# Batch 0 in two token halves: q and k by casting DMAs, and a first FFN block that begins on half its tokens

## The chip, the cores and the metric

One core of a Trainium2 chip. The metric is the device time of one launch in microseconds (us). Most runs of one kernel agree within 1%; all comparisons below are between runs of the state "fast", and a run that fell in the slower state (more than 1.5% above the fastest run of the same kernel) is named where it matters.

The kernel before had a median of 302.28 us (302.11 to 304.18, 3 runs). Over all rounds of this study, on several chips, it lay between 301.7 and 306.7 us, so each experiment is compared with the runs of the kernel before *of the same rounds*. Ratios are the mean time of one kernel's fast runs over that of the other's fast runs of the same rounds, so they are not quite the ratio of the medians quoted. Where two experiments of different rounds are compared by their times, chip and round differ too, and a difference of 1 us or less says nothing.

## The reference

```python
# B, H, S, Nb, D = 8, 8, 576, 16, 64 ; 4608 tokens, d_model 512, d_ff 768
k_all = concat([beacon_k, k], axis=2)          # 16 beacon columns, seen by every query
scores = q @ k_all.T / sqrt(D)                 # causal over the 576 own tokens
a = softmax(scores);  x = a @ v_all            # per batch and head
x = x.transpose(0, 2, 1, 3).reshape(B * S, H * D)
h = max(max(x @ w1, x @ w2), x @ w3)           # the FFN, three matrices in, maximum, one out
out = h @ w_out
```

(Cut: the set-up of the random inputs and the type conversions. Inputs and output are fp32.)

## The kernel before

Everything runs in bf16 on one core. Two heads are a *pair*, four pairs a batch, two pairs a *quad*. For each pair, q and k are loaded, cast, transposed on TensorE ("turned") and copied into `qT` and `kT`. The scores come in four groups; ScalarE (ACT) takes the exponentials, GpSimd or VectorE masks them, TensorE multiplies with v (PV) and with a column of ones. ACT inverts the sums (Ln, then Exp), VectorE multiplies into `xT`. The FFN takes blocks of 512 tokens: 22 units a block, 18 for w1, w2, w3 and 4 for w_out, doled out between the attention steps by a pacing formula. In batch 0 there is no FFN product to put between.

```python
def start():
    keep_busy(15)                              # dummy matmuls, to warm TensorE's clock
    next_load(); load_beacons(0, 1, bk32_0, nc.scalar); next_load(10)
    cast_piece(0, 0, by_dve); cast_piece(0, 1, by_act)
    ...                                        # turn pair 0, copy it out, turn the beacons
at_step(1, 0, C(cast_v, 0, 0, by_pool))        # GpSimd's work, by (pair, score group)
at_step(2, 0, L(load_w, 0, 0, d_ff))           # w0 asked for: after the start
...
at_step(4, 1, C(cast_v, 1, 0, by_pool))        # batch 1's values: cast here
at_step(4, 2, C(cast_v, 1, 1, by_pool))
at_step(5, 0, C(cast_pair, 7, by_pool, by_pool))
fine_at = {                                    # TensorE's work between batch 0's score groups
    (0, 0): [L(turn_apart, 1, 0)], (0, 1): [L(turn_apart, 1, 1)],
    ...
    (2, 0): [L(emit_pv, 0, 0, 0, 2)], (2, 1): [L(emit_pv, 0, 0, 2, 4), finish_pv],
    (2, 2): [L(keep_busy, 2, 320, True)],
    ...
    (4, 0): [L(turn_apart, 5, 0), L(turn_apart, 5, 1), L(emit_pv, 1, 0), finish_pv],
}
for p in range(NPAIR):                         # the loop, cut
    for s, gs in enumerate(steps(p)):
        ...                                    # scores, masks, PV
        if not fine and s == 0: place_beacons(p + 1, by_pool)
        emit_ffn(allowed)
        if not fine and s == 1: turn_pair(p + 1, by_act)   # in the PV banks
        ...
        finish_pv()
```

The softmax here doesn't subtract the row's maximum and nothing guards it: scores larger than these inputs give would overflow.

Of the kernel before, what the change touches and what calls it, by code (L numbers as in the profile page):

```python
# [16 lines left out]
def kernel(  # L17
# [13 lines left out]
    nc = tc.nc  # L31
# [17 lines left out]
    PR = 9  # L49
    PP = S // PR  # L50
    P_NINE = 4
# [18 lines left out]
    groups = [  # L70
# [5 lines left out]
    NG = len(groups)  # L76
    g_width = [sum(q1 - q0 for _, q0, q1 in pieces) for pieces in groups]
    g_base = [2 * sum(g_width[:gi]) for gi in range(NG)]
    AT_W = 2 * sum(g_width)
    assert max(g_width) <= 512  # L80
# [9 lines left out]
    st_pool = ctx.enter_context(tc.tile_pool(name="st", bufs=9))  # L90
    pair_pool = ctx.enter_context(tc.tile_pool(name="pair", bufs=3))
    v_pool = ctx.enter_context(tc.tile_pool(name="v", bufs=2))
# [25 lines left out]
    make_identity(nc, ident)  # L118
# [7 lines left out]
    for i in range(NT):  # L126
        z = const.tile([128, NKP], BF16, name=f"kT{i}")
        nc.vector.memset(z[:, NK:NKP], 0.0)
        kTs.append(z)
    nc.vector.memset(ones, 1.0)  # L130
    tri = const.tile([128, 128], BF16, name="tri")
    nc.gpsimd.memset(tri, 1.0)
    nc.gpsimd.affine_select(
        out=tri,
        in_=tri,
        compare_op=ALU.is_ge,
        fill=0.0,
        base=0,
        pattern=[[1, 128]],
        channel_multiplier=-1,  # L140
    )
# [19 lines left out]
    def load_pair(p, k_queue=None):  # L161
        b, g, j0 = place(p)
        hs = slice(head(g, j0), head(g, j0) + 2)
        st = new_stage(("pair", p))
        for i, (src, queue) in enumerate(((q, nc.sync), (k, k_queue or nc.sync))):
            if p < P_NINE:
                queue.dma_start(
                    out=st[:, i * PR * D : (i + 1) * PR * D],
                    in_=src[b, hs].rearrange("h (p r) d -> (h p) (r d)", r=PR),
                )  # L170
            else:
                queue.dma_start(
                    out=st[0:QP, i * NQ2 : (i + 1) * NQ2].rearrange("p (h x) -> p h x", h=2),
                    in_=src[b, hs].rearrange("h (p r) d -> p h (r d)", r=QR),
                )

    def cast_piece(p, i, cast):
        st = stage["pair", p]
        if p < P_NINE:
            t16 = pair_pool.tile([128, PR, D], BF16, name=f"t16{i}")  # L180
            cast(
                t16.rearrange("x r d -> x (r d)"), st[:, i * PR * D : (i + 1) * PR * D]
            )
        else:
            t16 = pair_pool.tile([QP, QR, 2, D], BF16, name=f"p16{i}")
            cast(  # L186
                t16.rearrange("p r h d -> p h r d"),
                st[0:QP, i * NQ2 : (i + 1) * NQ2].rearrange("p (h r d) -> p h r d", h=2, r=QR),
            )
        stage["pair16", p, i] = t16  # L190
# [63 lines left out]
    def turn_beacons(b0, b1, src):  # L254
        n = Nb * (b1 - b0)
        ps = ffn_psum.tile([128, PPB, n], BF16, name="fps")
        for pi in range(PPB):
            nc.tensor.transpose(
                ps[:, pi],
                src[:, 2 * pi : 2 * pi + 2].rearrange("p h d -> p (h d)"),  # L260
                ident[0:n, 0:n],
            )
        if b0 == 0:
            by_act(kTs[0][:, 0:Nb], ps[:, 0, 0:Nb])
        by_act(bT[:, :, Nb * b0 : Nb * b1], ps)
# [31 lines left out]
    def turn(p, i, ps):  # L297
        src = stage.pop(("pair16", p, i))
        if p >= P_NINE:
            for r in range(QR):  # L300
                nc.tensor.transpose(  # L301
                    ps[:, r * QP : (r + 1) * QP],
                    src[:, r].rearrange("p h d -> p (h d)"),
                    ident[0:QP, 0:QP],
                )
            return
        for r in range(PR):
            for e in range(2):
                hs = slice(64 * e, 64 * e + 64)
                nc.tensor.transpose(  # L310
                    ps[hs, r * PP : (r + 1) * PP],
                    src[hs, r],
                    ident[hs, hs],
                    tile_position=(64 * e, 64 * e),
                )

    def rows(p):
        return PR if p < P_NINE else QR

    def evac_q(p, ps, copy):  # L320
        copy(
            qTs[p % NT].rearrange("d (p r) -> d p r", r=rows(p)),
            ps.rearrange("d (r p) -> d p r", r=rows(p)),
# [6 lines left out]
    def evac_k(p, ps, copy):  # L330
        kT = kTs[p % NT]
        copy(  # L332
            kT[:, Nb:NK].rearrange("d (p r) -> d p r", r=rows(p)),
            ps.rearrange("d (r p) -> d p r", r=rows(p)),
# [9 lines left out]
    def turn_pair(p, q_copy):  # L344
        banks = [pv_bank(i, [128, 1024], BF16) for i in range(2)]
        for i in range(2):
            turn(p, i, banks[i][:, 0:S])
        evac_q(p, banks[0][:, 0:S], q_copy)
        evac_k(p, banks[1][:, 0:S], by_dve)
# [12 lines left out]
    def at_view(p, t, e, q0, q1):  # L362
        for gi, pieces in enumerate(groups):
            off = g_base[gi] + e * g_width[gi]
            for t_, lo, hi in pieces:
                if t_ == t and lo <= q0 and q1 <= hi:
                    return at[p][0 : k_rows[t], off + q0 - lo : off + q1 - lo]
# [3 lines left out]
    def both_heads(p, gi):  # L371
        W = g_width[gi]
        return at[p][:, g_base[gi] : g_base[gi] + 2 * W].rearrange("k (e c) -> k e c", e=2)

    def emit_scores(p, gi):
# [6 lines left out]
        for t, q0, q1 in groups[gi]:  # L382
# [12 lines left out]
            out=both_heads(p, gi), in_=ps[:, :, 0 : g_width[gi]], func=AF.Exp, scale=scale  # L395
        )

    def emit_masks(p, gi, dve=False):
        off = 0
        for t, q0, q1 in groups[gi]:  # L400
            n = k_rows[t]
# [28 lines left out]
    def emit_pv(quad, hf, first=0, last=len(passes), apart=False):  # L430
        b, g = divmod(quad, n_quad)
        v_sb = v_tiles[b]
        if first == 0:
# [6 lines left out]
        for part, bank, lo, ca, cb in passes[first:last]:  # L440
            qa, qb = hf * HALF + ca, hf * HALF + cb
            ts = [t for t in range(n_kt) if q_min[t] < qb]
            for t in ts:
                q0 = max(qa, q_min[t])
                for j in range(4):
                    lhsT = (
                        ones[0 : k_rows[t]]
                        if part == 0
                        else v_sb[0 : k_rows[t], t, head(g, j), part - 1 : D : 2]
# [12 lines left out]
    def finish_pv():  # L462
# [3 lines left out]
        b, g = divmod(quad, n_quad)  # L466
# [5 lines left out]
        c0 = b % RING * S + hf * HALF  # L472
        for part, bank, lo, ca, cb in passes[1:]:
# [5 lines left out]
        if g == n_quad - 1 and hf == 1:  # L479
            ready[0] = b  # L480
# [7 lines left out]
    def mm1_unit(tb, ft, i, pool, name):  # L488
        if ft == 0 and i == 0:
            hTs[tb] = ffn_h.tile([128, n_ft, TOKB], BF16, name="hT")  # L490
        hT = hTs[tb]
        ps = pool.tile([128, TOKB], FP32, name=name)
        c0 = tb * TOKB % (RING * S)
        n0 = min(TOKB, RING * S - c0)
        for x0, o0, n in ((c0, 0, n0), (0, n0, TOKB - n0)):
# [8 lines left out]
        if i == 0:  # L504
            (by_act if alone[0] else by_dve)(hT[:, ft, :], ps)  # L505
        else:
            nc.vector.tensor_max(hT[:, ft, :], hT[:, ft, :], ps)  # L507
# [23 lines left out]

    units = []
    for tb in range(n_tokb):
        last_b = (TOKB * (tb + 1) - 1) // S
        for i in range(3):
            for ft in range(n_ft):
                units.append((last_b, mm1_unit, (tb, ft, i)))
        for tt in range(TOKB // 128):
            units.append((last_b, mm2_unit, (tb, tt)))
    UPB = len(units) // n_tokb  # L540
    done = [0]

    def emit_ffn(limit, pool=None, name="fps"):
        if done[0] + 1 <= limit and done[0] < len(units) and units[done[0]][0] <= ready[0]:
            _, fn, args = units[done[0]]
            fn(*args, pool or ffn_psum, name)
            done[0] += 1
            return True
# [18 lines left out]
    loads = [L(load_pair, 0, nc.scalar), L(load_pair, 1, nc.scalar)] + load_pairs(2, 4)  # L567
    loads += [L(load_v, 0, 0), L(load_beacons, 1, B_PE, bk32_1), L(load_v, 0, 1)]
# [18 lines left out]
    def start():  # L587
        keep_busy(15)
        next_load()
        load_beacons(0, 1, bk32_0, nc.scalar)  # L590
        next_load(10)
        cast_piece(0, 0, by_dve)
        cast_piece(0, 1, by_act)
        stage.pop(("pair", 0))
        by_pool(bk16_0, bk32_0)
        next_load()
        q_ps = ffn_psum.tile([128, S], BF16, name="fps")
        k_ps = ffn_psum.tile([128, S], BF16, name="fps")
        turn(0, 0, q_ps)
        turn(0, 1, k_ps)  # L600
        evac_q(0, q_ps, by_act)
        evac_k(0, k_ps, by_dve)
        turn_beacons(0, 1, bk16_0)
        keep_busy(4)
        C(cast_pair, 1, by_pool, by_pool)()
# [5 lines left out]


    P_FINE = PPB + 1

    def steps(p):
        return [[gi] for gi in range(NG)] if p < P_FINE else [[0, 1], [2, 3]]

    at_step(0, 0, C(cast_pair, 2, by_pool, by_pool))
    at_step(0, 1, C(cast_pair, 3, by_pool, by_pool))
    at_step(1, 0, *[L(emit_masks, 0, gi) for gi in range(NG)])  # L620
    at_step(1, 0, C(cast_v, 0, 0, by_pool))
    at_step(1, 1, C(cast_v, 0, 1, by_pool))
    at_step(1, 2, L(by_pool, bk16_1, bk32_1))
    at_step(1, 3, C(cast_pair, 4, by_pool, by_pool))
    at_step(2, 0, L(load_w, 0, 0, d_ff))
    at_step(2, 2, C(cast_pair, 5, by_pool, by_pool))
    at_step(3, 2, C(cast_pair, 6, by_pool, by_pool))
    at_step(3, 3, L(load_w, 1, 0, d_ff))
    at_step(4, 1, C(cast_v, 1, 0, by_pool))
    at_step(4, 2, C(cast_v, 1, 1, by_pool))  # L630
    at_step(5, 0, L(load_w, 2, 0, d_ff))
    at_step(5, 0, C(cast_pair, 7, by_pool, by_pool))
    at_step(6, 0, L(load_w_out))
# [6 lines left out]

# [118 lines left out]
```

## Time and profile before

| | kernel before |
|---|---|
| median | 302.28 us |
| span in the profile, first to last instruction | 301.2 us |
| first exponential | 7.85 us |
| first FFN product | 31.48 us |
| end of FFN block 0 | 70.95 us |
| from there to the end | 230.25 us, TensorE busy 225.8 |

"End of FFN block 0" is the end of the fourth w_out unit in TensorE's timeline. It is a good mark: after it TensorE is full, so whatever a change of the start brings must show as an earlier mark. The lines of the profile are in the prediction.

### The profile page before, as it was taken

To read this page: it belongs to the slowest core of one execution; us is meant where nothing else is said; L and a number is where in the kernel's file an instruction comes from. 1 tells how busy PE (TensorE), PEld (TensorE's weight loads), DVE (VectorE), ACT (ScalarE), POOL (GpSimd) and SP (SyncE) were. 2 spreads that over 40 slices of the span, in tenths; PEclk is the share of its full clock that TensorE was granted. 3 is DMA by queue.
4 is the path that set the end of the run, shared out by engine and by line. 5 is a ranking of instruction groups with operands and counts; after the bars stand their busy time and mean duration, and the time that the engine had idled before them with its cause. 6 is when DMAs were issued, how large, how long until landed. Compare 5 with 4: busy or idle time off the path is not lost.

```text
span 301.2 us, 8622 instructions
## 1 busy us (share of the span) xinstructions
PE 285.2 (95%) x3563; PEld 147.8 (49%) x3563; DVE 174.2 (58%) x330; ACT 143.1 (48%) x220; POOL 128.6 (43%) x261
## 2 busy tenths in 40 slices
PE   7797849999999999999999999999999999999995
PEld 4454325454454545454445777545454544444442
DVE  2966525656766476646564656465646575275373
ACT  3786635573555464636463646354645531400300
POOL 3876294455666583465455543652243210000000
PEclk9979989999999999999999999999999999999999
DMA  7999999999899999999999999557512001103003
GB/s 258 211 255 216 208 239 239 216 227 216 177 311 180 265 223 262 191 188 253 291 202 177 249 236 201 113 141 209 115 44 104 2 2 70 72 0 116 25 2 139
DMA packets 83095, 51.55 MB, mean 171 GB/s; under 512 B 62064, under 2 KB 76656, under 8 KB 83056
## 3 DMA queue, kind: packets, MB, share of 16 engines
q1 hardware_dynamic: 80976, 47.23, 70.4%
q0 software_dynamic: 1648, 3.15, 5.5%
q8 instruction: 28, 0.46, 0.7%
q10 hardware_dynamic: 432, 0.62, 0.6%
q14 instruction: 11, 0.09, 0.1%
HBM read 35.13 MB, written 14.22 MB: 164 GB/s over the span
## 4 chain that ended last, share of the span: by engine, by line
PE 81%; DMA 9%; SPq 3%; DVE 2%; POOL 2%; issue 1%; ACT 0%; POOLq 0%; DVEq 0%
PE fps L497 41%; PE fps L514 13%; PE pv L451 11%; PE sc L385 8%; DMA st<-in_v_dram 5%; PE sc L497 5%; PE sc L514 2%; DMA st<-in_q_dram 2%; DMA st<-in_k_dram 2%; SPq L249 1%; SPq L213 1%; PE pv L301 1%; DVE kT L332 1%; POOL v_sb L229 1%; POOL at_sb L410 1%
## 5 line engine op out<-in xcount | busy, mean ns | idle before, releaser
L394 ACT ACTIVATE at_sb<-sc 128x992 bf16<-128x992 f32 (+3 forms) x128 | 103.5, 862 | 99.1 <-PE sc L385 99.1
L497 PE MATMUL fps<-xT,w_sb 128*128 128x512 bf16 (+1 forms) x648 | 140.2, 357 | 1.2 <-ACT at_sb L394 1.2
L497 PEld LDWEIGHTS <-w_sb 128*128 128x128 bf16 x720 | 65.8, 98 | 71.5 <-issue 15.4
L507 DVE TENSOR_TENSOR hT<-hT,fps 128x512 bf16<-128x512 bf16 x96 | 65.8, 686 | 46.0 <-PE fps L497 45.8
L410 POOL TENSOR_SCALAR_AFFINE_SELECT at_sb<-at_sb 128x256 bf16<-128x256 bf16 (+2 forms) x145 | 52.5, 384 | 90.7 <-ACT at_sb L394 89.2
L186 POOL CAST p<-st 96x768 bf16<-96x768 f32 x56 | 44.8, 825 | 9.2 <-DMA q_dram<-p 5.3
L514 PE MATMUL fps<-w_out_sb,hT 128*128 128x512 bf16 x180 | 41.8, 379 | 0.0
L505 DVE CAST hT<-fps 128x512 bf16<-128x512 f32 x42 | 29.0, 690 | 19.8 <-PE fps L497 19.7
L385 PE MATMUL sc<-qT,kT 64*128 64x288 bf16 (+4 forms) x384 | 35.8, 284 | 2.9 <-POOL kT L328 1.9
L522 DVE COPY y<-fps 128x512 f32<-128x512 f32 x30 | 20.7, 690 | 27.9 <-PE fps L514 25.1
L514 PEld LDWEIGHTS <-hT 128*128 128x128 bf16 x216 | 20.5, 98 | 25.0 <-DVE hT L507 1.3
L474 DVE TENSOR_TENSOR xT<-pv,recip 128x288 bf16<-128x288 f32 (+2 forms) x93 | 27.3, 349 | 4.6 <-ACT recip L471 4.4
L451 PE MATMUL pv<-at_sb,v_sb 128*32 128x192 bf16 (+4 forms) x1352 | 28.9, 232 | 0.0
L385 PEld LDWEIGHTS <-kT 64*128 64x128 bf16 x384 | 13.8, 94 | 27.9 <-issue 19.4
L451 PEld LDWEIGHTS <-v_sb 128*32 128x32 bf16 (+1 forms) x1408 | 24.9, 98 | 3.0 <-issue 1.9
L229 POOL CAST v_sb<-st 128x512 bf16<-128x512 f32 (+2 forms) x26 | 21.5, 844 | 9.8 <-DMA st<-in_v_dram 9.8
L451 PE MATMUL pv<-at_sb,ones 128*32 128x288 bf16 (+4 forms) x492 | 17.9, 258 | 2.9 <-POOL at_sb L410 2.1
L497 PE MATMUL sc<-xT,w_sb 128*128 128x512 bf16 x72 | 18.5, 379 | 0.0
L469 ACT ACTIVATE lnd<-pv 128x288 f32<-128x288 f32 x31 | 12.9, 415 | 8.2 <-PE pv L451 8.2
L451 PEld LDWEIGHTS <-ones 128*32 128x32 bf16 (+1 forms) x512 | 11.1, 96 | 10.2 <-issue 8.0
L507 DVE TENSOR_TENSOR hT<-hT,sc 128x512 bf16<-128x512 bf16 x12 | 8.3, 688 | 12.5 <-PE sc L497 12.2
L505 ACT CAST hT<-sc 128x512 bf16<-128x512 f32 x6 | 3.5, 586 | 23.7 <-PE sc L497 23.7
(47 smaller groups left out, 114.6 us busy)
## 6 DMA issues: line engine op xcount, KB each, us to landing
st<-in_q_dram SPq DMA_DIRECT2D x32, 288.0 KB, 5.7
out_dram<-y SPq DMA_DIRECT2D x36, 256.0 KB, 2.8
st<-in_k_dram SPq DMA_DIRECT2D x30, 288.0 KB, 6.1
st<-in_v_dram SPq DMA_DIRECT2D x24, 256.0 KB, 6.7
w_sb<-in_moe_w_dram POOLq DMA_DIRECT2D x6, 384.0 KB, 9.2
q_dram<-p SPq DMA_DIRECT2D x16, 144.0 KB, 2.6
k_dram<-p SPq DMA_DIRECT2D x16, 144.0 KB, 2.5
st<-in_v_dram SPq DMA_DIRECT2D x8, 224.0 KB, 6.4
```

The source lines that it names most:

```text
L186: cast(t16.rearrange("p r h d -> p h r d"), st[0:QP, i * NQ2 : (i + 1) * NQ2].rearrange("p (h r d) -> p h r d", h=2, r=QR),)
L229: cast(v_sb[0:n, t:t1].rearrange("p t h d -> p (t h d)"), st[0:n, (t - t_lo) * H * D : (t1 - t_lo) * H * D],)
L385: nc.tensor.matmul(ps[:, e, off : off + q1 - q0], kT[hs, 128 * t : 128 * t + 128], qT[hs, q0:q1], start=True, stop=True, tile_position=(64 ...
L394: nc.scalar.activation(out=both_heads(p, gi), in_=ps[:, :, 0 : g_width[gi]], func=AF.Exp, scale=scale)
L410: nc.gpsimd.affine_select(out=view, in_=view, compare_op=ALU.is_ge, fill=0.0, base=x0, pattern=[[0, 2], [1, hi - lo]], channel_multiplier=-1,)
L451: nc.tensor.matmul(ps[bank][32 * j : 32 * j + 32, lo + q0 - qa : lo + qb - qa], lhsT, at_view(PPQ * quad + j // 2, t, j % 2, q0, qb), star ...
L474: nc.vector.tensor_mul(xT[:, 2 * g + part - 1, c0 + ca : c0 + cb], ps[bank][:, lo : lo + cb - ca], recip[:, ca:cb],)
L497: nc.tensor.matmul(ps[:, o0 : o0 + n], w_in[i][:, ct, 128 * ft : 128 * (ft + 1)], xT[:, ct, x0 : x0 + n], start=(ct == 0), stop=(ct == n_c ...
L505: (by_act if alone[0] else by_dve)(hT[:, ft, :], ps)
L507: nc.vector.tensor_max(hT[:, ft, :], hT[:, ft, :], ps)
L514: nc.tensor.matmul(ps, hT[:, ft, 128 * tt : 128 * (tt + 1)], w_out_sb[:, ft, :], start=(ft == 0), stop=(ft == n_ft - 1),)
L522: nc.vector.tensor_copy(y, ps)
```

## The change

The intent is to fill the first 31 us, in which TensorE waits for exponentials and has no FFN product. Batch 0 is cut in two halves of 288 tokens. The first halves of all four pairs go first, so that x is complete for 288 tokens early and FFN block 0 can begin with half units (256 tokens of w1 and w2) while the second halves are still in attention. Most of batch 0's q and k, and w0 after them, come by casting DMAs on GpSimd's software queue, so no engine casts them (w0 came that way before too, but was asked for at 20.63 us). From pair 4 on the loop is also reordered: pairs are turned in a score bank instead of the PV banks, and the beacon columns are copied into `kT` by VectorE instead of GpSimd.

```diff
-    keep_busy(15)
-    next_load() ... cast_piece(0, 0, by_dve) ... turn(0, 0, q_ps)
+    keep_busy(12)
+    load_half(0, 0, nc.sync); load_half(0, 1, nc.scalar)
+    load_half(1, 0, nc.sync); load_beacons(0, 1, bk32_0, nc.scalar); load_half(1, 1, nc.scalar)
+    load_quad(1, 0); load_quad(0, 1); load_quad(1, 1)     # casting DMAs, GpSimd
+    load_w(0, 0, d_ff)                                    # w0, right behind them
+    next_load(9)                      # batch 0's values, beacons, pairs 4 to 6, batch 1's values, pair 7
 ...
+    first_steps = [
+        ((0, 0), [T(2, 0, False)]),
+        ((1, 0), [M(0, 0, True), T(3, 0, True), C(cast_v, 0, 0, by_pool)]),
+        ((2, 0), [M(1, 0), T(0, 1, False)]),
+        ((3, 0), [T(1, 1, True), M(2, 0, True), M(3, 0)]),
+        ((0, 1), [M(0, 1), L(load_w, 1, 0, d_ff)]),
+        ((0, 2), [T(2, 1, False), M(0, 2)]),
+        ((0, 3), [M(0, 3, True), P(0, 0)]),
+        ((1, 1), [M(1, 1), finish_pv]),
+        ((1, 2), [P(1, 0, True), M(1, 2)]),
+        ... ((2, 2), [M(2, 1), F(2), M(2, 2, True)]), ...  # F(2): two FFN half units
+    ]
 ...
-    at_step(4, 1, C(cast_v, 1, 0, by_pool)); at_step(4, 2, C(cast_v, 1, 1, by_pool))
+    at_step(5, 0, C(cast_v, 1, 0, by_pool)); ... at_step(5, 1, C(cast_v, 1, 1, by_pool))
 ...
+        if tb == 0:
+            spans = [(0, 0, 0, MID), (1, 0, 0, MID), (0, need, MID, TOKB), (1, need, MID, TOKB)]
 ...
-        if not fine and s == 0: place_beacons(p + 1, by_pool)
+                    place_beacons(p + 1, by_dve)
```

(Cut: the same idea carried through the loads, transposes, masks and score groups of batch 0, and the order of the loop. `T` turns a half pair, `M` masks, `P` is a PV product, `F(n)` emits n FFN half units, `C` is a GpSimd cast and the next load.)

## The prediction

> **What bounds the kernel now.** I read first the busy shares and the strip of 40 slices, to see which engine fills which part of the time.
>
> ```profile
> PE 285.2 (95%) x3563; PEld 147.8 (49%) x3563; DVE 174.2 (58%) x330; ACT 143.1 (48%) x220; POOL 128.6 (43%) x261
> ...
> PE   7797849999999999999999999999999999999995
> ...
> PEclk9979989999999999999999999999999999999999
> DMA  7999999999899999999999999557512001103003
> ```
>
> One slice is 7.5 us. TensorE is full from the seventh slice to the last; only the first six have holes. So I then cut the run into windows at the events that matter: first scores (7.4), end of the last exponential of batch 0 (24.9), first FFN product (31.48), the end of the holes (44.67), the end of FFN block 0 (70.95), the last product. Columns: window, its length, busy time of PE, PEld, DVE, ACT, POOL, granted clock, DMA share, GB/s.
>
> ```profile
> 0.00:7.40 7.40, 5.61 (x59) 3.16 (x59) 1.71 (x8) 2.88 (x5) 2.29 (x10) 1.00 0.76 255
> 7.40:24.90 17.50, 14.86 (x317) 8.83 (x316) 13.43 (x30) 14.25 (x22) 13.89 (x24) 0.90 1.07 231
> 24.90:31.48 6.58, 3.76 (x128) 2.45 (x129) 4.21 (x13) 4.22 (x9) 2.75 (x6) 1.00 1.13 216
> 31.48:44.67 13.19, 9.17 (x100) 4.38 (x100) 4.83 (x8) 6.09 (x9) 8.82 (x20) 0.93 1.08 226
> 44.67:70.95 26.28, 25.95 (x348) 12.99 (x344) 15.24 (x30) 14.51 (x23) 12.75 (x27) 0.97 1.13 230
> 70.95:297.50 226.55, 225.81 (x2620) 115.99 (x2620) 134.13 (x244) 101.13 (x156) 88.13 (x177) 1.00 0.69 153
> ```
>
> From 70.95 on, TensorE is busy 225.81 of 226.55 us: nothing is to be had there unless work is removed, and the change removes none. All the room is before 44.67, where ACT does the exponentials of batch 0 (14.25 busy of 17.5 us) and no FFN product runs until 31.48. The chain of waits up to 60 us says why: a load of batch 1's values, then GpSimd in its order.
>
> ```profile
> 19.76 15.94 DMA st<-in_v_dram
> 35.77 0.08 issue
> 35.85 1.46 POOL v_sb L229
> ...
> 40.15 0.14 POOL kT L328
> ```
>
> That load took 15.94 us. GpSimd waited for it, then had casts and masks to do before it copied the beacon columns into kT at 40.10. In the timeline TensorE is held by exactly these two things:
>
> ```profile
> 40.35 0.54 PE L385 MATMUL sc<-qT,kT 64*128 64x288 bf16 x8 [1.89 <-POOL kT L328]
> ...
> 43.31 0.57 PE L451 MATMUL pv<-at_sb,ones 128*32 128x176 bf16 x6 [2.11 <-POOL at_sb L410]
> ```
>
> **What the Trainium skill says.** (1) "DMA: Bandwidth & Descriptors", section SWDGE vs HWDGE vs iDMA: a cast during a DMA can be issued from GpSimd only, where software writes the descriptors. The trace agrees on the cost to GpSimd: the six casting weight loads took 528 to 673 ns of POOL each and 7.0 to 11.9 us to land. (2) The same page, Queues, rings and completion order: each DMA engine goes round-robin between its queues, a packet at a time. The trace fits: while four weight loads were under way, the value load beside them took 15.94 us against a median of 6.7. (3) "SBUF — State Buffer", Who interferes with whom: VectorE in a two-port mode and GpSimd exclude each other from a shared port for a whole instruction. The small copy into kT shows something like it: 186 to 194 ns on GpSimd, but 158, 518 (median) and 2169 ns on VectorE. (4) "TensorE: Matmul & The Clock Gate", Part 1: a quiet TensorE drops to half clock. The granted clock was 0.64 in the window 16 to 20 us.
>
> **The change part by part.**
> *Start.* Pairs 0 and 1 load half as much first (0.59 MB for both pairs instead of 1.18), so transposes can begin nearly 1 us earlier than 5.37. But VectorE now casts the beacons in its order, and they landed at 5.9; and pair 1's transposes stand ahead of pair 0's scores. First exponential: about 7.4 instead of 7.85.
> *Loads.* Pairs 2 and 3 and all second halves come by six casting DMAs (0.295 MB read each, 1.77 MB), then w0 (1.57 MB) behind them on the same queue; w0 had been asked for at 20.63. In 4 to 8 us before, with large runs alone, 380 GB/s arrived; w0 and w1 beside value loads took 14 us for 3.15 MB read, 225 GB/s. At 200 to 225 from 3 us on: the three quads land at about 7, 10 and 13 us, w0 at about 20, w1 at about 27. The first FFN product can thus run at 20 to 21 instead of 31.48. The six issues cost GpSimd about 6 x 0.65 = 4 us, at a time when it was waiting.
> *ACT in batch 0.* Two exponentials of 992 and 736 columns take 1.67 us in the timeline, 0.97 ns a column. Batch 0 has 3328 columns a pair, 3.2 us; four pairs 12.9. Three inversions (0.41 + 0.44 each) add 2.55: 15.4. ACT was busy 81% of the time in 7.4 to 24.9 before. The new order has more waits in it (TensorE's order puts each PV, which waits for masks and cast values, ahead of later scores, and the FFN products wait for w0 and for the first half of x). I choose 72%: 15.4 / 0.72 = 21.4, so the last exponential of batch 0 ends at 28.8 (24.9 before, with no FFN product among them). With the transposes of pair 4 and two FFN half units (1.2 us), **pair 4 starts at about 30**, with 4 of block 0's 22 units already done.
> *From pair 4 to the end of block 0*, all on TensorE, durations by start to start in the packed stretch: 6 x 0.48 + 5 x 0.45 scores = 5.1; 6 turns x 0.51 = 3.1; PV 3 x 1.61 + 2 x 0.79 = 6.4; FFN 14 units x 0.88 + 4 x 1.33 = 17.6. Sum 32.2. The stall at 38 to 43 goes: the beacon copy is now VectorE's, and batch 1's values are asked for in the start, needed about 12 us after pair 4. I leave 1 us for new waits. Block 0 ends at 30 + 32.2 + 1 = 63.2 against 70.95: **7.75 us earlier**.
> *After that* the pacing formula gives the same FFN units beside the same pairs (22 due at the end of pair 9's first step in both, 145.75 at the end of pair 31), so the 226.55 + 3.7 us that follow should stay. Turning pairs in the score banks instead of the PV banks, and multiplying later, only reorders; TensorE is full there, so I put it at 0 +- 1.5. 302.3 - 7.8 = **294.5 us**.
>
> **The rivals.**
> *A: the casting DMAs are the new wait.* They are small runs (768 bytes in), mixed with the values' 256-byte runs and with w0, behind six software issues. For it: DMA share is at 1 all through the start, and the total before w1 has landed is not smaller than before. Against: the first 4 MB need only some 10 to 11 us at 380 GB/s. If each quad is 4 us late, TensorE, which works in order, holds everything: pair 4 at 34 to 36, a time of 298 to 301.
> *B: VectorE and GpSimd block each other.* Batch 0 now gives VectorE the beacon copies, half-width evacuations and many masks, just while GpSimd casts values. For it: the 2169 ns copy. Against: before, VectorE made five such copies in this phase too. Worth 1 to 3 us: 296 to 298.
> *C: the gain is handed back between pair 4 and pair 10*, because w1, w2, w_out or batch 1's values are not there when TensorE comes sooner. w_out is issued behind pair 7's casts, at perhaps 38, took 13.7 us to land, and is needed at about 54. For it: the load side was full (DMA share 1.13 up to 70.95). Against: about 10 us of slack at w2. 3 to 6 us back: 297 to 300.
> *D: better than I think.* If ACT stays at 81% as before, pair 4 starts near 27.5: 291 to 292.
>
> **Range and chances.** A, B and C each take from the gain, D adds. I put the middle at 294.5 and 8 of 10 between 288.5 and 299.5. Faster by 2% means under 296.2: the middle passes it by only 1.7 us, so faster 0.67, within 2% 0.30. Slower by 2% would need the start to lose 6 us net, against one in which no FFN product runs for 31 us: 0.03.
>
> **What would show it right or wrong.** Right: first FFN product at 20 to 22 us, pair 4's scores at 28 to 32, end of block 0 at 61 to 66, then about 230 us of full TensorE to the end. A shows as TensorE or VectorE waiting for a transpose whose source is a quad tile, or for w0, before 25 us. B shows as kT copies of over 1 us on VectorE. C shows as TensorE waits on weights or on masks behind a load between 30 and 60 us. If the stretch after block 0 is not within 1.5 us of 230, the claim that the reordering is neutral is wrong.

## The result, and the profile after

The changed kernel took 312.49 us (312.07 to 312.99, 4 runs) against 303.23 (302.11 to 304.90, 4 runs) for the kernel before in the same rounds: ratio 1.0301, 95% interval 1.0240 to 1.0362. **It is 3% slower; the prediction said 2.6% faster.** (Its own output check is not on record; the kernels below, most of them edits of it, all gave correct results.)

First the page of the changed kernel: busy time of TensorE, then its strip, its clock and the DMA engines in 40 slices of 7.8 us.

```profile
PE 291.4 (94%) x3566; PEld 155.4 (50%) x3566; DVE 178.4 (57%) x363; ACT 144.4 (46%) x221; POOL 129.6 (42%) x257
...
PE   7848895998999999999999999999999999999994
...
PEclk9999999799999999999999999999999999999999
DMA  8999999993976899979997999878202000202003
```

The third slice now is at 4. Beware of the clock strip (the clock that the throttle granted to TensorE, in tenths of full speed): it shows full speed at the start, but the profile holds no clock record before 34.0 us. The durations tell another story, as will be seen. Next the windows of the changed kernel at the prediction's marks: first exponential, first FFN product, pair 4's scores, end of FFN block 0, end (columns as in the prediction).

```profile
0.00:8.55 8.55, 6.31 (x52) 3.38 (x54) 3.25 (x18) 2.48 (x6) 6.66 (x16) 1.00 0.90 156
8.55:28.27 19.72, 13.76 (x207) 7.35 (x207) 8.17 (x29) 11.03 (x16) 7.82 (x18) 1.00 1.12 215
28.27:40.18 11.91, 10.48 (x137) 6.79 (x138) 6.18 (x18) 4.47 (x8) 4.90 (x8) 1.00 1.17 224
40.18:81.61 41.43, 35.95 (x571) 22.47 (x572) 23.65 (x52) 25.26 (x38) 22.48 (x43) 0.96 0.97 196
81.61:311.10 229.49, 224.85 (x2609) 115.45 (x2608) 137.14 (x250) 101.19 (x155) 87.77 (x172) 1.00 0.63 149
```

The last row settles one thing: after block 0 the changed kernel needs 229.49 us, the kernel before 230.25. **The whole loss is ahead of that mark**, which moved from 70.95 to 81.61 us. Against the prediction the first FFN product is 7 us late (28.27 for 20 to 22), pair 4 is 10 us late (40.18 for 30), and the stretch from there to the end of block 0 took 41.43 us instead of 33.2.

Who made whom wait? In the chain of waits of the changed kernel one piece is far larger than any other; it is shown here with what follows it:

```profile
4.20 15.28 DMA st<-in_v_dram
19.48 0.05 issue
19.53 0.62 POOL v_sb L258
20.15 0.34 POOL at_sb L450
```

A load of batch 0's values ends at 19.48. GpSimd waits for it, and behind that cast, in the same queue, stand masks of the exponentials. In the timeline of the changed kernel TensorE's first PV product waits for exactly these masks:

```profile
20.53 0.85 PE L494 MATMUL pv<-at_sb,ones 128*32 128x288 bf16 x10 [4.28 <-POOL at_sb L450]
```

And ACT, which sets the pace of batch 0, waits for scores that stand behind this PV product in TensorE's order. The list of waits up to 36 us, "engine, what it could not start, for whom: total us, times, longest", for the kernel before and then for the changed one:

```profile
ACT at_sb L394 <- PE sc L385: 5.2, 5, 1.8
```

```profile
ACT at_sb L431 <- PE sc L422: 15.0, 7, 6.6
```

So ACT was busy 15.3 of the 29.1 us between the first and the last exponential of batch 0: 53%, where 72% was predicted.

A second new stall lies later, beside batch 1's value casts. First GpSimd's and then VectorE's timeline of the changed kernel, and what TensorE did:

```profile
49.48 1.46 POOL L258 CAST v_sb<-st 128x1536 bf16<-128x1536 f32 x1
50.89 1.60 POOL L215 CAST p<-st 96x768 bf16<-96x768 f32 x2
```

```profile
50.21 3.14 DVE L364 COPY kT<-bT 128x16 bf16<-128x16 bf16 x1
```

```profile
53.43 2.98 PE L553 MATMUL fps<-xT,w_sb 128*128 128x256 bf16 x16 [2.04 <-DVE hT L561]
```

The copy of 16 beacon columns, 153 ns at its shortest, took 3.14 us while GpSimd ran its casts and then issued w_out's load (52.44 to 53.29); the evacuation of an FFN bank stood behind it on VectorE, and TensorE waited 2.04 us for that bank.

### The profile page after: what moved, and what is told of

Same layout as the page of the kernel before. It is cut to its first block, busy times and chain, and to the rows that moved or that the text cites. A ratio compares the mean times of both kernels' runs of the same rounds, so it can differ in the third digit from the quotient of the medians.

```text
span 311.1 us, 8625 instructions
## 1 busy us (share of the span) xinstructions
PE 291.4 (94%) x3566; PEld 155.4 (50%) x3566; DVE 178.4 (57%) x363; ACT 144.4 (46%) x221; POOL 129.6 (42%) x257
## 4 chain that ended last, share of the span: by engine, by line
PE 84%; DMA 6%; DVE 5%; ACT 2%; issue 1%; POOL 0%; DVEq 0%; ACTq 0%
PE fps L553 33%; PE pv L494 13%; PE sc L553 12%; PE fps L570 11%; PE sc L422 8%; DMA st<-in_v_dram 5%; PE sc L570 4%; PE sc L329 2%; DVE kT L368 1%; DMA h<-in_q_dram 1%; DVE kT L364 1%; DVE y L578 1%; ACT at_sb L431 1%; DVE xT L526 1%; PE fps L494 1%
## 5 line engine op out<-in xcount | busy, mean ns | idle before, releaser
L431 ACT ACTIVATE at_sb<-sc 128x928 bf16<-128x928 f32 (+5 forms) x128 | 104.0, 861 | 102.9 <-PE sc L422 100.6
L553 PE MATMUL fps<-xT,w_sb 128*128 128x512 bf16 (+1 forms) x580 | 123.7, 347 | 4.4 <-DVE hT L561 2.3
L563 DVE TENSOR_TENSOR hT<-hT,fps 128x512 bf16<-128x512 bf16 (+1 forms) x82 | 52.8, 648 | 34.3 <-PE fps L553 33.8
L553 PE MATMUL sc<-xT,w_sb 128*128 128x512 bf16 (+1 forms) x188 | 43.1, 356 | 0.0
L422 PE MATMUL sc<-qT,kT 64*128 64x288 bf16 (+5 forms) x400 | 38.1, 294 | 2.0 <-ACT qT L357 2.0
L561 DVE CAST hT<-fps 128x512 bf16<-128x512 f32 (+1 forms) x44 | 26.9, 618 | 17.5 <-PE fps L553 17.5
L563 DVE TENSOR_TENSOR hT<-hT,sc 128x512 bf16<-128x512 bf16 x32 | 22.0, 688 | 16.6 <-PE sc L553 16.2
L494 PE MATMUL pv<-at_sb,v_sb 128*32 128x288 bf16 (+5 forms) x1376 | 30.1, 235 | 0.0
L494 PEld LDWEIGHTS <-ones 128*32 128x32 bf16 (+2 forms) x512 | 11.2, 98 | 12.6 <-issue 11.0
L570 PE MATMUL sc<-w_out_sb,hT 128*128 128x512 bf16 x60 | 14.8, 379 | 0.3 <-DVE hT L563 0.3
```

Source lines behind the costliest of these rows:

```text
L422: nc.tensor.matmul(ps[:, e, off : off + q1 - q0], kT[hs, 128 * t : 128 * t + 128], qT[hs, q0:q1], start=True, stop=True, tile_position=(64 ...
L431: nc.scalar.activation(out=both_heads(p, gi), in_=ps[:, :, 0 : g_width(p, gi)], func=AF.Exp, scale=scale)
L494: nc.tensor.matmul(ps[bank][32 * j : 32 * j + 32, lo + q0 - qa : lo + qb - qa], lhsT, at_view(PPQ * quad + j // 2, t, j % 2, q0, qb), star ...
L553: nc.tensor.matmul(ps[:, o0 : o0 + n], w_in[i][:, ct, 128 * ft : 128 * (ft + 1)], xT[:, ct, x0 : x0 + n], start=(ct == 0), stop=(ct == n_c ...
L561: (by_act if alone[0] else by_dve)(h, ps[:, 0 : hi - lo])
L563: nc.vector.tensor_max(h, h, ps[:, 0 : hi - lo])
```

## The experiments

Eighteen kernels ran, all with a correct result. Four theories of the loss were tried first:

- **Clock**: the first phase runs at half clock because its matmuls are sparse and there are only 12 dummies.
- **Values starved**: w0, asked for in the start, takes DMA time from batch 0's values.
- **Shared port**: VectorE's beacon copies collide with GpSimd's casts from pair 4 on.
- **Loop body**: turning pairs in a score bank brings new waits.

### Clock: warm, before12

`warm` adds dummy matmuls so that TensorE never cools before the first PV product:

```diff
-        keep_busy(12)
+        keep_busy(20)
-        ((0, 0), [T(2, 0, False)]),
+        ((0, 0), [T(2, 0, False), L(keep_busy, 5, 320, True)]),      # and in four more turns
-        ((0, 3), [M(0, 3, True), P(0, 0)]),
+        ((0, 3), [M(0, 3, True), L(keep_busy, 34, 320, True), P(0, 0)]),
```

> The changed kernel with 20 dummy products at its start (12), five more after each of five turns of batch 0, and 34 ahead of the first PV. Theory C (clock): TensorE never reached full clock before 33.6 us for want of dense work; with these it is at full clock by 6 us, the transposes of 96 columns fall from 283 to about 200 ns and the scores of 288 columns from 418 to 290 ns, the values' stall stays (first PV still ends its wait near 20.5), and 4 to 6 us are saved: 306.5 to 308.5. Theory V (only the values' load counts): less than 2 us saved, over 310.5.

Measured: 312.09 us, ratio 1.0275 (1.0224 to 1.0326). It saved 0.4 us. Up to the first PV product the clock did what was wanted. Twelve transposes in the changed kernel, then in `warm`, by TensorE's timeline:

```profile
10.39 0.69 PE L344 MATMUL pv<-ident,quad 96*64 96x96 bf16 x12
```

```profile
10.47 0.45 PE L344 MATMUL pv<-ident,quad 96*64 96x96 bf16 x12
...
17.43 4.79 PE L390 MATMUL fps<-busy 128*128 128x320 bf16 x34
22.15 0.52 PE L494 MATMUL pv<-at_sb,ones 128*32 128x288 bf16 x12
```

The mean duration of a score matmul of 288 columns was 418 ns in the changed kernel at 8 to 12 us and 293 ns in `warm`. Like matmuls stayed that long in the changed kernel (412 to 422 ns at 22 to 30 us) and took 293 ns from 34 us on. So it did run at half clock up to about 34 us, whatever its clock strip says. But the values were cast at 19.38 in `warm`, as late as before, and the first PV product came at 22.15. The time set free went into waiting. As the *first* cause, the clock falls. Later `warm` did not stay warm: at 28 to 30 us, with its first FFN products, its granted clock was 0.53.

`before12` takes three dummies out of the kernel before (`keep_busy(15)` to `keep_busy(12)`):

> The kernel before with 12 dummy products at its start instead of 15, nothing else. Theory C: three dummies decide the clock; it stays at half clock past 5 us, up to where the FFN makes it dense, transposes of 64 columns and scores of 288 columns (293 ns) become about 1.4 times as long, and the time rises by 2 to 5 us, to 305 to 308. If 12 are enough here, the time stays within 0.5% and the sparse work, not the dummies, is what keeps the changed kernel cold.

Measured: 303.84 us, ratio 0.9998 (0.9948 to 1.0049). Twelve dummies are enough there; it is the later, sparser work that lets the changed kernel stay cold, not their number (`sc_ahead_warm` below has 20 and none in the turns, and was at 0.51 at 12 to 16 us).

### Values starved: w0late, w0late_warm, quad_hw

`w0late` asks for w0 only after the cast of batch 0's first values:

```diff
         load_quad(1, 1)
-        load_w(0, 0, d_ff)
         next_load(9)
-        ((1, 0), [M(0, 0, True), T(3, 0, True), C(cast_v, 0, 0, by_pool)]),
+        ((1, 0), [M(0, 0, True), T(3, 0, True), C(cast_v, 0, 0, by_pool), L(load_w, 0, 0, d_ff)]),
```

> The changed kernel with w0's load issued after the casts of batch 0's first values and no longer ahead of them. Theory V: the third value tile lands near 14 to 15 us instead of 19.5, the first PV waits under 1 us, 3 to 5 us saved: 307.5 to 309.5, still at half clock. Theory C alone: the time is spent elsewhere at half clock, under 2 us saved.

Measured: 309.04 us, ratio 1.0175 (1.0123 to 1.0228), 3.4 us better than the changed kernel, as expected. GpSimd's and TensorE's timelines of `w0late`:

```profile
15.50 0.61 POOL L258 CAST v_sb<-st 128x512 bf16<-128x512 f32 x1 [3.26 <-DMA st<-in_v_dram]
```

```profile
17.63 0.84 PE L494 MATMUL pv<-at_sb,ones 128*32 128x288 bf16 x10 [1.08 <-POOL at_sb L450]
```

The third value cast came at 15.50 instead of 19.53, the wait of the first PV product fell from 4.28 to 1.08 us, and block 0 ended at 77.2 instead of 81.6. w0's early load cost more than it gave: no wait for w0 had been seen at all.

`w0late_warm` joins this with the dummies of `warm` (10 instead of 34 ahead of the first PV):

> Both together (10 dummies ahead of the first PV). If C and V are separate causes, the sum of their gains, 8 to 11 us: 302 to 305, as the kernel before. If they are the same gap seen twice, no better than the better of the two.

Measured: 309.05 us, ratio 1.0167 (1.0107 to 1.0227). A miss: the dummies added nothing even here. But this is no test of a start at full clock either: from 26 to 30 us `w0late_warm` ran at 0.50, and its pair 4 came at 37.54 us, that of `w0late` at 36.45.

`quad_hw` asks whether the software queue itself is at fault. It is `w0late`, but the quads come in fp32 on SyncE's hardware queue and GpSimd casts them:

```diff
-            nc.gpsimd.dma_start(out=t16..., in_=half_source(g, h, i, 0, 4))   # casts on the way
+            nc.sync.dma_start(out=st[0:QP, ...], in_=half_source(g, h, i, 0, 4))
+            by_pool(t16..., st[0:QP, ...])                                    # later
```

> w0late with the six casting DMAs replaced by loads of fp32 on the sync queue, in order with the values (quads 1 and 0's second half ahead of the first values, the last quad after them), cast on GpSimd. To be compared with w0late (309.0). Theory V in its narrow form (the software queue takes turns with the values' short runs and holds them back): the third value tile lands by 12 us instead of 15.5 and 1.5 to 3 us are saved, 306 to 307.5. If only the bytes count: within 1 us of 309.

Measured: 313.90 us, ratio 1.0321 (1.0281 to 1.0362), 4.9 us slower than `w0late`. The third value cast came at 15.25, hardly sooner than the 15.50 of `w0late`: the casting DMAs were not what still held the values back. The last quad was cast at 18.29 and TensorE waited 2.5 us for one of those casts. So of the two ways tried the casting DMAs are the better one; what delayed the values was w0 beside them.

### From pair 4 on: oldloop, beac_pool, w0late_oldloop

`oldloop` gives the changed kernel the loop body of the kernel before from pair 4 on (beacon copies on GpSimd, pairs turned in the PV banks, sums inverted and multiplied at the step's end). `beac_pool` takes back one line of it only:

```diff
-                        place_beacons(p + 1, by_dve)
+                        place_beacons(p + 1, by_pool)
```

> The changed kernel with the body of the loop from pair 4 on as it was before: beacon copies on GpSimd, pairs turned in the PV banks at a pair's second step, sums inverted and multiplied at the end of a step. Batch 0's start stays as changed. Theory L (the reordered loop is not neutral): in the changed kernel TensorE waits 0.34, 0.99, 0.30, 2.04, 0.34 and 1.30 us between pair 4 and the end of block 0, on copies out of the score banks and on a VectorE copy of 3.1 us, and falls to half clock once more; with the old body 4 to 6 us are saved, 306.5 to 308.5, and from pair 4's scores to the end of block 0 it takes 35 to 37 us instead of 41.4. If the loop is neutral, as the prediction had it, within 1 us of 312.5.

> The changed kernel with only the beacon copies of that loop back on GpSimd. Theory S (shared port): the 3.1 us copy on VectorE near 50 us is gone, and with it the 2.04 us wait of TensorE and the fall to half clock at 54 us (1.5 to 2 us more): 308.5 to 310.5. If the copy only waits for something else that stays, within 1 us of 312.5, and TensorE shows a like wait near 51 us.

Measured: `oldloop` 310.07 us, ratio 1.0196 (1.0159 to 1.0234); `beac_pool` 309.20 us, ratio 1.0159 (1.0124 to 1.0193). The copies of `beac_pool`, by engine (shortest, median and longest in ns):

```profile
L364 POOL COPY kT<-bT x11: 188/197/198, 40.5 to 115.6; 128x16 bf16<-128x16 bf16 x11
L364 DVE COPY kT<-bT x4: 153/160/161, 8.0 to 37.4; 128x16 bf16<-128x16 bf16 x4
```

No copy is long any more and TensorE's wait of 2.04 us is gone. The one line is worth all that the old body is worth, so the score-bank turns are not a loss: that theory falls. One caution: in the profiled run of `beac_pool` the values also happened to be cast at 17.75 instead of 19.53, which an edit after 40 us cannot cause. From pair 4 to the end of block 0 it took 38.8 us instead of 41.4, so the copies, with the fall of the clock behind their wait, account for about 2.6 of the 3.3 us.

`w0late_oldloop` (both edits):

> w0 issued late and the old loop body, both. If the two are separate, 309.0 less 4 to 6: 303 to 305, level with the kernel before.

Measured: 307.43 us, ratio 1.0104 (1.0070 to 1.0139), 2.4 to 4.4 us short of what was expected.

### Both waits mended, then the clock: w0late_beac, w0late_beac_warm, w0late_beac_few

`w0late_beac` has the edits of `w0late` and `beac_pool`. `w0late_beac_warm` adds dummies through the whole start: 20 first, 5 in each turn, 10 ahead of the first PV product, and 7 and 4 ahead of the first FFN product. `w0late_beac_few` leaves out the dummies in the turns and keeps 6 ahead of the PV product.

> w0late and beac_pool together. The starved values (w0late alone saved about 3.4 us against the changed kernel) and the copies on the shared port (beac_pool alone saved about 3.3 us) lie in different stretches, the first before pair 4, the second between pair 4 and the end of FFN block 0. If both theories hold the gains add: 305.5 to 306.5 us, ratio to before about 1.005 to 1.009. If the two are one delay seen twice, it stays at 308 to 309 us.

> w0late_beac with dummy matmuls at the start, in the turns, before the first PV product and at two places before the first FFN product, to hold TensorE at full clock through the whole start. Clock theory: with the waits shorter the clock is what is left, 303 to 304 us. Rival (what the runs warm and w0late_warm point to): the waits set the phase, the same as w0late_beac within 0.7 us.

> w0late_beac_warm without the five dummies in each turn of batch 0 (kept: 20 at the start, 6 before the first PV product, 7 and 4 later). If the turns' own transposes keep TensorE warm, the dummies there only cost: about 1 us faster than w0late_beac_warm (305.6), 304 to 305. If TensorE cools in the turns: between w0late_beac_warm and w0late_beac, 306 to 307.5.

| run | median us | ratio to before | 95% |
|---|---|---|---|
| w0late_beac | 307.92 | 1.0153 | 1.0097 to 1.0208 |
| w0late_beac_warm | 305.63 | 1.0079 | 1.0016 to 1.0143 |
| w0late_beac_few | 308.02 | 1.0084 | 1.0004 to 1.0163 |

The two mended waits together saved 4.6 us of the median, not the 6.7 of their sum (by the ratios 4.5, not 8.1). On top of them the dummies are worth 2.3 us, in the same rounds. `w0late_beac_warm` is the first of these kernels that stayed at full clock from 8 us to pair 4: its score matmuls of 288 columns took 293 ns and its half-unit FFN matmuls 273 ns where `w0late_beac` took up to 418 and 414. Yet the gain is not made there. Pair 4's first scores in TensorE's timeline, `w0late_beac` and then `w0late_beac_warm`:

```profile
35.97 0.90 PE L422 MATMUL sc<-qT,kT 64*128 64x288 bf16 x8
```

```profile
36.11 0.54 PE L422 MATMUL sc<-qT,kT 64*128 64x288 bf16 x8
```

They come at the same time: what the faster matmuls saved in the start went into dummies and waiting even now. The kernels part behind this mark. There `w0late_beac` fell to half clock once more (0.50 at 36 to 38 us), and its FFN block 0 ended at 75.61 instead of 74.21; the two profiled runs differ by 1.34 us. So what the dummies were worth in these two runs lies behind pair 4's start, where TensorE stayed warm. Whether the clock was worth nothing in `warm` and `w0late_warm` because larger waits hid it, or because their dummies did not hold it that far, these runs do not separate.

`w0late_beac_few` points the same way but settles nothing. Its three fast runs (the fourth was in the slow state; the median in the table counts it) took 304.94, 306.97 and 309.07 us with mean granted clocks of 0.989, 0.978 and 0.967. But the recorded mean is a weak witness, since it leaves out what precedes the first record: two runs of `w0late_beac` took 307.87 and 306.97 us with 1.000 and 0.961.

A balance of TensorE up to the end of block 0 shows where the time sits. The windows up to that mark of the kernel before, of the changed kernel and of `w0late_beac_warm` (first figures: length, busy time of TensorE):

```profile
0.00:70.95 70.95, 59.34 (x945) 31.80 (x947) 39.42 (x87) 41.94 (x64) 40.51 (x84) 0.95 1.07 231
```

```profile
0.00:81.61 81.61, 66.50 (x960) 39.99 (x962) 41.25 (x113) 43.24 (x66) 41.86 (x85) 0.98 1.03 201
```

```profile
0.00:74.21 74.21, 64.67 (x1010) 40.64 (x1016) 38.52 (x107) 43.24 (x66) 42.55 (x91) 1.00 1.10 217
```

The same windows for the dummies alone gave 6.86, 4.09 and 13.26 us. So:

| us, to the end of FFN block 0 | before | after | w0late_beac_warm |
|---|---|---|---|
| end of block 0 | 70.95 | 81.61 | 74.21 |
| TensorE, real work | 52.48 | 62.41 | 51.41 |
| TensorE, dummies | 6.86 | 4.09 | 13.26 |
| TensorE, idle | 11.61 | 15.11 | 9.54 |

The changed kernel's real work is stretched by 11 us (62.41 against 51.41), mainly by half clock. That looks like the whole loss and is not: where the stretching was taken away in the start, it turned into dummies and waiting. Dummies and idle together, the time for which TensorE has nothing to do, are 18.5 us before and 22.8 us in the mended kernel. **The halves give TensorE FFN work earlier, and yet its holes grow.**

### What is the early FFN half worth? nosplit and before_halves

`w0late_beac_nosplit` has FFN block 0 in whole units, none before pair 4 (`if tb == 0:` to `if tb < 0:` in the list of units). `w0late_beac_warm_nosplit` does the same to `w0late_beac_warm`, with dummies in the places of the eight early half units. `before_halves` takes only the split into the kernel before: w1 and w2 of block 0 in 24 half units.

```diff
+        if tb == 0:
+            spans = [(0, 0, HT), (1, 0, HT), (0, HT, TOKB), (1, HT, TOKB), (2, 0, TOKB)]
```

> w0late_beac with FFN block 0 in whole units after the attention of all its tokens, so no FFN product before pair 4. If the early FFN half fills TensorE time that would be idle: 2 to 3 us slower than w0late_beac (308 to 309). If its 24 half units' extra cost (about 0.08 us each, 2 us in all) and its early need of w0 eat what it fills: within 1 us of w0late_beac, or faster.

> w0late_beac_warm, but FFN block 0 in whole units and none before pair 4; in the places of the eight early half units stand dummies of the same length, so that TensorE stays warm and pair 4 starts when it did (36 us). If early FFN work is worth its TensorE time: eight half units (3.7 us) less progress at pair 4, 16 later half units whole again (16 x 0.08 = 1.3 us back): about 2.4 us slower, ratio about 1.016. If after pair 4 TensorE has waits that absorb them: within 1 us of w0late_beac_warm, ratio 1.006 to 1.010.

> The kernel before with only FFN block 0's first two weight matrices in 24 half units (256 tokens each) instead of 12 whole ones times two, in the order of the changed kernel, nothing moved. If a half unit costs what the timeline of the changed kernel shows (0.54 against 0.46 us, 48 half units of 0.08): up to 3.8 us slower, ratio 1.007 to 1.013. If the waits of that stretch hide it: within 0.7 us, ratio 0.998 to 1.002.

(The last expectation has a slip: it counts 48 half units. There are 24, so its own working gives 24 x 0.08 = 1.9 us, 0.6%.)

| run | median us | ratio to before | 95% |
|---|---|---|---|
| w0late_beac_nosplit | 308.01 | 1.0161 | 1.0108 to 1.0214 |
| w0late_beac_warm_nosplit | 307.79 | 1.0180 | 1.0126 to 1.0234 |
| before_halves | 304.35 | 1.0053 | 1.0011 to 1.0094 |

Cold, the early FFN half is worth nothing (307.92 with, 308.01 without). With TensorE warm it is worth 2 to 3 us (1.0079 against 1.0180, in different rounds, with intervals that just overlap), near the 2.4 expected. And the split alone costs the kernel before 0.53%, 1.6 us. Its price is in TensorE's timelines; three half units of `w0late_beac_warm`, then two whole ones of its version without the split:

```profile
41.24 1.72 PE L553 MATMUL fps<-xT,w_sb 128*128 128x256 bf16 x12
42.89 0.30 PE L422 MATMUL sc<-qT,kT 64*128 64x288 bf16 x2
```

```profile
41.59 1.90 PE L553 MATMUL fps<-xT,w_sb 128*128 128x512 bf16 x8
43.42 0.54 PE L422 MATMUL sc<-qT,kT 64*128 64x288 bf16 x8
```

Start to start, a half unit takes (42.89 - 41.24) / 3 = 0.55 us, half a whole one (43.42 - 41.59) / 4 = 0.46.

### The order of TensorE's queue: sc_ahead, sc_ahead_warm, sc_ahead_warm_nosplit

What keeps pair 4 at 36 us in the mended kernel? ACT still waited 10.6 us for scores. A last theory: whole PV products and FFN units stand ahead of the next scores, where the kernel before splits its PV products around them. `sc_ahead` is `w0late_beac` with this order:

```diff
-        ((0, 3), [M(0, 3, True), P(0, 0)]),
-        ((1, 1), [M(1, 1), finish_pv]),
-        ((1, 2), [P(1, 0, True), M(1, 2)]),
+        ((0, 3), [M(0, 3, True)]),
+        ((1, 1), [P(0, 0, last=2), M(1, 1)]),
+        ((1, 2), [P(0, 0, first=2), finish_pv, M(1, 2)]),
 ...                                   # likewise P(0, 1); pair 4 cast and turned one or two steps earlier
```

> w0late_beac with another order of TensorE in batch 0: each PV product is split and moved behind the next group of scores, and pair 4's cast and transposes come a step or two earlier. Theory: what is left of the loss is ACT idle because whole PV products and FFN units stand ahead of the next scores (3.1, 1.6, 2.9 and 3.1 us of ACT's idle time in w0late_beac); of these some half should go, pair 4 starts at 32 to 33 instead of 36 and the time is 304.5 to 306 against 307.9. Rival (order is not what holds ACT): within 1 us of w0late_beac.

> sc_ahead with 20 dummies at the start, 6 ahead of the first PV product and 4 ahead of the first FFN units. If order and clock are two separate costs: 301.5 to 303.5. If warmth again only fills waits: the same as sc_ahead.

> sc_ahead_warm with FFN block 0 in whole units, none before pair 4. If the early half block is worth something once the order lets ACT run: 1 to 3 us slower than sc_ahead_warm. If not even then: within 1 us or faster.

| run | median us | ratio to before | 95% |
|---|---|---|---|
| sc_ahead | 306.95 | 1.0085 | 1.0040 to 1.0129 |
| sc_ahead_warm | 306.89 | 1.0099 | 1.0042 to 1.0156 |
| sc_ahead_warm_nosplit | 306.77 | 1.0039 | 0.9956 to 1.0122 |

The theory is not borne out in this form. Pair 4's scores came at 36.8, not at 32 to 33, and the span in the profile was 305.0 us, that of `w0late_beac` 305.1 (in its fastest run). By the medians `sc_ahead` is 1 us better, by the ratios 2 us, in different rounds and with overlapping intervals; so a small gain is open. The PV wait was gone, but two others had taken its place in TensorE's timeline of `sc_ahead`:

```profile
25.37 1.87 PE L553 MATMUL fps<-xT,w_sb 128*128 128x256 bf16 x8 [1.68 <-DVE xT L526]
...
33.40 0.60 PE L553 MATMUL fps<-xT,w_sb 128*128 128x256 bf16 x4 [1.46 <-DVE qT L357]
```

The FFN product caught up with the multiplication that makes its x, then with the copy that empties its bank. `sc_ahead_warm` missed too (301.5 to 303.5 was expected if order and clock were separate costs), but its dummies did not hold the clock (0.51 at 12 to 16 us, 0.50 at 26 to 28), so it does not test the order at full clock. The third kernel's three fast runs (a fourth was slow; the median in the table counts it) spread from 303.3 to 307.7 us with the clock between 0.991 and 0.967: inconclusive.

### What the kernel before had to give: before_v1late

The prediction counted on removing a stall at 38 to 43 us, where GpSimd's masks stand behind a cast that waits for batch 1's values. In the changed kernel that stall is indeed gone. Does one need the change for it? `before_v1late` is the kernel before with these lines moved, nothing else (each takes with it the request for the next load):

```diff
-    at_step(4, 1, C(cast_v, 1, 0, by_pool))
-    at_step(4, 2, C(cast_v, 1, 1, by_pool))
-    at_step(5, 0, C(cast_pair, 7, by_pool, by_pool))
+    at_step(5, 1, C(cast_v, 1, 0, by_pool))
+    at_step(5, 1, C(cast_v, 1, 1, by_pool))
+    at_step(5, 1, C(cast_pair, 7, by_pool, by_pool))
```

> The kernel before with one edit: GpSimd's casts of batch 1's values moved behind the masks and the beacon copy of pair 6, so that these don't stand in GpSimd's queue behind a cast that waits for values landing at about 36 us. If that stall (seen at 38 to 43 us in the profile of before) costs what it shows: 299.5 to 300.5 us, ratio about 0.988 to 0.991. If another wait takes its place: 303 to 304, unchanged.

Measured: **300.11 us, ratio 0.9890 (0.9833 to 0.9947)**, the fastest kernel of the study: it beats the changed kernel by 4% and the kernel before by 1.1%. GpSimd's and then TensorE's timeline of `before_v1late`, to be held against the two TensorE lines at 40.35 and 43.31 in the prediction:

```profile
38.08 0.19 POOL L328 COPY kT<-bT 128x16 bf16<-128x16 bf16 x1
...
40.69 2.58 POOL L229 CAST v_sb<-st 128x1536 bf16<-128x1536 f32 x3
```

```profile
41.31 0.55 PE L385 MATMUL sc<-qT,kT 64*128 64x288 bf16 x8 [0.16 <-DVE kT L332]
41.79 0.40 PE L451 MATMUL pv<-at_sb,ones 128*32 128x288 bf16 x12
```

The copy runs at 38.08 instead of 40.10, the casts come after it, and TensorE's waits of 1.89 and 2.11 us are gone. FFN block 0 ends at 68.39 us instead of 70.95.

## Why the prediction was wrong

The mechanism named as the gain was there, but every step that would have delivered it was too optimistic, and the price of the split was not in the sum.

**The step that failed first: "Loads".** It worked out when the quads and w0 would land and did not time the load that decides: batch 0's values, which go on another queue at the same time and whose cast stands ahead of masks in GpSimd's order. The quads were nearly right: TensorE waited 0.58 and 0.24 us for them. w0's place behind the quads was taken for a gain ("w0 at about 20"). In fact no wait for w0 was seen, and its early load pushed the values' cast from 15.5 to 19.5 us. Measured by `w0late`: 3.4 us. Rival A had the mechanism (a new wait made by the casting queue) but looked for it on the quads and on w0; in `quad_hw`, without casting DMAs for the quads, the values came no sooner.

**"Start": first exponential at 7.4 became 8.55**, later than the 7.85 before. TensorE waited 0.91 us for VectorE's cast of the beacons, and pair 1's transposes ahead of pair 0's scores took 0.69 us at half clock. A small term, but with the wrong sign.

**"ACT in batch 0": 72% busy became 53%.** The prediction chose 72% because it knew of waits but could not size them. ACT's waits for scores rose from 5.2 to 15.0 us. Of the 10 us by which pair 4 was late, w0's early load explains 3.7 (40.18 against 36.45 in `w0late`); the rest is this term and the late start, which no run separates. Even with values, port and clock mended it was 15.4 busy of 24.8 us, 62%, with pair 4 at 36.1 instead of 30.

**"From pair 4 to the end of block 0": 32.2 + 1 us became 41.43.** Of the 8.2 us, TensorE's busy time is 35.95 - 32.2 = 3.75 and idle time 5.5 - 1 = 4.5. Idle: rival B's collision, to which the prediction gave 1 to 3 us and only as a rival; without the copies on VectorE this stretch was 2.6 us shorter, and `beac_pool` saved 3.3 in all. Busy: the FFN term counted half units at half the price of whole ones; they cost 0.55 instead of 0.46, and `before_halves` puts the split at 1.6 us. Part of this stretch also ran at half clock again, right after the wait of 2.04 us (0.61 at 54 to 56 us, 0.53 at 56 to 58).

**The clock was named and not counted.** The prediction cited a granted clock of 0.64 at 16 to 20 us before, and had no term for it after. The changed kernel ran at half clock to about 34 us. Warming the start alone brought next to nothing (`warm`: 0.4 us; pair 4 at 35.97 cold and 36.11 warm once both waits were mended). Dummies after which the clock also held behind pair 4 were worth 2.3 us.

**Does it add up?** The loss is 3.0%, 9.1 us. The two waits mended together give back 4.6 us (1.0301 to 1.0153), the dummies on top of them 2.2 (to 1.0079), and the half units cost 1.6 in the kernel before: 8.4 of 9.1. This is a balance, not a proof. The last term was measured in another kernel, and in the mended one taking the split out made it slower. The two waits are not independent of each other (6.7 us singly). And each ratio is uncertain by about 0.5%, 1.5 us.

**What was right.** After block 0 the reordered loop is neutral, as predicted (229.5 against 230.25 us), the stall at 38 to 43 us is gone, and eight half units are done when pair 4 starts. Rival C did not happen: no wait for weights stood out between 30 and 60 us.

**What stays open.** Why the mended kernel does not *gain*. Its dummies and idle time are 22.8 us against 18.5 before, though it has FFN work from 26.8 us on and the kernel before from 31.5. Splitting the PV products around the scores helped little, if at all (`sc_ahead`); what the runs show is that each mended wait was followed by one on the next link of the same chain (scores, exponential, mask, PV, inversion, multiplication, FFN). Which order, if any, would let halves pay was not found.

## What to carry to other kernels

Before moving loads forward, list every transfer that is in flight at that time and ask which engine stands in order behind each: here the transfer that decided was one that the prediction did not time. A small movement of work that frees a queue held by a late load (1.1%, three lines) can be worth more than a restructuring that fills the same hole from another side, so try the small one alone first. And work put into a stall is worth only what the next link of the chain leaves of it: mend waits one at a time and look again. Then see from the timeline where a gain arises: full clock in the start did not move the mark of pair 4, and the end of FFN block 0 came 1.4 us sooner because of what lay between the two.

## What the Trainium skill lacked or had wrong

- "TensorE: Matmul & The Clock Gate", Part 1, Seeing it yourself: the page warns that the records of clock transitions can be unreliable, but not that nothing need be recorded of the time before the first of them. In the changed kernel that was at 34.0 us, and the windows before it read 1.00, while score matmuls of 288 columns took 418 ns against 293 ns in a kept-warm run. Durations of like matmuls tell the clock there.
- The same page, Back-to-back issue gap, gives about 131 ns a matmul for a sustained stream at 512 columns and calls 216 ns the isolated gap. Here eight such FFN matmuls in a stream took 1.83 us start to start, 229 ns each; at 256 columns it was 137 ns, more than half. For 256 columns the page has no figure of a sustained stream; by these two numbers the same work costs about 20% more in halves.
- "SBUF — State Buffer", Who interferes with whom: the loser of the shared port blocks for a whole instruction of the other engine; the page does not say whether it gets the port before the next one. The 128x16 copy on VectorE began at 50.21 us and ended at 53.35. GpSimd worked without a gap from 49.48 to 53.29: a cast of 1.46 us, two of 1.60 us together and the issue of w_out's load. So the copy seems to have been held over several instructions.
- "DMA: Bandwidth & Descriptors", Queues, rings and completion order, has the round of queues by packets but no figure for what a load of short runs loses to it. Here the last of batch 0's first value tiles was cast at 19.53 us with w0 on the software queue beside it and at 15.50 us without.
